# Cluster attention, experts and a bilinear layer on one core: expert order, small norms, last tile and a skipped branch

## The chip, the cores and the metric

The kernel runs on one core of a Trainium2 chip. The core has TensorE (matrix multiply; the profile shows matmuls as PE and weight loads as PEld), VectorE (DVE), ScalarE (ACT), GpSimd (POOL) and SyncE (SP), which only issues DMAs and handles semaphores here. Each engine works through its own queue of instructions in order; engines wait for one another by semaphores. The metric is the device time of one execution in microseconds.

## The reference

Three stages, all in float32. In the first, q and k (2 batches, 8 heads, 768 rows of 64) are given to the nearest of 16 centroids per head, and a row of q sees only rows of k of the same cluster.

```python
mask = q_assign[:, :, :, None] == k_assign[:, :, None, :]
scores = np.where(mask, scale * q @ k.T, -1e9)
attn = softmax(scores) ; x = attn @ v          # 1536 tokens x 512
expert_idx = argmax(normed(x) @ normed(expert_emb).T / tau)
gate = softmax(logits)[expert_idx]             # 8 experts
x = gate * (relu(x @ w1[e]) @ w2[e])           # each token by its expert e
out = ((x @ w_a) * (x @ w_b)) @ w_out          # 512 -> 1536 -> 512
```

## The kernel before

**Attention** goes over 8 pairs of heads in 96 steps of 128 query rows (SPP = 12 steps a pair). A step's scores go to PSUM, VectorE takes the row maximum (L601), ScalarE the exponential (L606), TensorE turns it (L621), ScalarE and VectorE copy it back (L625, L627), and after three steps the product with v follows (L648). Beside it, generators prepare the next pair: split_rows (with GpSimd's L389 and L390), prep_gen, and in the first pair setup_rest, which normalizes the expert embeddings.

A norm's reciprocal is made by `root_recip` (L265 to L286): three Newton rounds on a [rows, 1] column, each a reciprocal, a multiply by half (L279) and a multiply-add (L281), all on VectorE. It serves the centroids (128 rows), the embeddings (8 rows) and, on a 128x12 tile, the gates.

**Weights** come in chunks of 512x512. Chunks of turns with a wide tile go through four raw buffers of two quarter-chunks each: SP loads one (`load_raw`, L140 to L160), ScalarE makes the rounded high part (L207), VectorE the low part (L208), which frees the buffer. Chunks of the two narrow turns are loaded whole (`load_whole`, L172 to L180). The first four raw loads are issued during attention, at the steps of L872.

**Experts** are worked in eight turns. Expert 0 is the first turn; the others are ordered by how many tokens they have, and a turn's place in the order sets how wide its tile is (WIDTHS) and how many products it takes (KINDS). `ranks` (L1046) works the order out from the counts `cnt`: key, a comparison, its sum (pbase), then the table `at` and `turn_i`, the expert of each turn. SP reads turn_i into a register for the loads of later turns (L165), ScalarE for the gather of a turn's tokens (`load_xe`, L1134 to L1137). `limits` gives each expert's capacity and `most`, the largest overflow.

The main loop has an index G: 8 turns of 8 steps, then the bilinear layer. In a step TensorE does layer1(G) (L1169 in a wide turn) and layer2(G - 2) (L1286), ScalarE and VectorE make the hidden tile's two parts (L1246, L1247), and `split_some` splits as many quarter-chunks as a ramp and the room allow. At a turn's end the result ys is copied (L1299) and stored by SP (`put_rows`, L1310). Before the loop, the first turn's tile is taken from PSUM: cnt (L1017), two copies (L1020) and two subtractions (L1022).

At G = 5 stands `rare` (L1172): if an expert has more tokens than its turn's width, every engine goes through an arm that works the overflow in tiles of 128 tokens. All five engines load `most` into a register and branch (L1175). An engine that skips the arm goes through a short skipping arm instead: it waits for its own semaphores (and those of DMAs that it issued) to reach their count and adds what the arm would have added. With these inputs the arm is skipped. Its DMAs are issued by SP.

**Bilinear layer.** 1536 tokens in four chunks; at its end each 128-token tile is scaled by its gate and scattered to the output by GpSimd (`leave`, L1384 to L1397). The order of all instructions is the order in which this program writes them; no planner changes it.

Of the kernel before, what the change touches and what calls it, by code (L numbers as in the profile page):

```python
# [16 lines left out]
ALU = mybir.AluOpType  # L17
# [5 lines left out]
P = 128  # L23
# [25 lines left out]
def kernel(  # L49
# [215 lines left out]
    def root_recip(pool, shape, n2, name):  # L265

        g = pool.tile(shape, I32, name=name + "_g", bufs=1)
        nc.vector.tensor_scalar(out=g, in0=n2.bitcast(I32), scalar1=1, scalar2=None, op0=ALU.logical_shift_right)
        half = pool.tile(shape, F32, name=name + "_h", bufs=1)
        nc.vector.tensor_scalar(out=half, in0=n2, scalar1=0.5, scalar2=None, op0=ALU.mult)  # L270
        yield
        nc.vector.tensor_scalar(out=g, in0=g, scalar1=float(0x1FC00000), scalar2=None, op0=ALU.add)
        s0 = g.bitcast(F32)
        r = pool.tile(shape, F32, name=name + "_r", bufs=1)
        for _ in range(3):
            yield
            nc.vector.reciprocal(r, s0)
            yield
            nc.vector.tensor_mul(r, r, half)  # L279
            yield  # L280
            nc.vector.scalar_tensor_tensor(out=s0, in0=s0, scalar=0.5, in1=r, op0=ALU.mult, op1=ALU.add)  # L281
        yield
        nc.vector.tensor_scalar(out=s0, in0=s0, scalar1=1e-6, scalar2=None, op0=ALU.add)
        yield
        nc.vector.reciprocal(r, s0)
        return r  # L286
# [570 lines left out]
    for s in range(nst):  # L857
# [11 lines left out]
            nc.sync.dma_start(out=dst, in_=src)  # L869
        if i == SPP // 2 and pp > 0 and pp + 1 < NP:  # L870
            load_v(pp + 1)
        if s in (4 * SPP + 1, 4 * SPP + 3, 4 * SPP + 7, 4 * SPP + 9):  # L872
            load_raw()
        if s == (NP - 1) * SPP:
            near_open()
# [136 lines left out]
    def new_x(key, dt=F32R):  # L1012
        return big.tile([P, 2, DC, CAP], dt, tag="xT", name=f"xT_{key}", bufs=2)

    split_some(2)
    cnt = left.tile([P, NE, 1], F32, name="cnt")
    nc.vector.tensor_sub(cnt, cnt_p.rearrange("p (e o) -> p e o", o=1), ebase.rearrange("p o e -> p e o"))  # L1017
    xT_t[0] = new_x(0)
    for u in range(2):
        nc.scalar.copy(xT_t[0][:, 0, 2 * u:2 * u + 2, :], near_t["ps"][u])  # L1020
    for u in range(2):
        nc.vector.tensor_sub(xT_t[0][:, 1, 2 * u:2 * u + 2, :], near_t["ps"][u], xT_t[0][:, 0, 2 * u:2 * u + 2, :])  # L1022
    cnt_i = left.tile([1, NE], I32, name="cnt_i")
    most = left.tile([1, 1], I32, name="most")
    prod_ = left.tile([P, NE, OVM], F32, name="prod")
# [20 lines left out]
    def ranks():  # L1046

        nc.vector.scalar_tensor_tensor(out=key, in0=cnt.rearrange("p e o -> p o e"), scalar=float(NE), in1=iota_e, op0=ALU.mult, op1=ALU.add)
        nc.vector.memset(key[:, :, 0:1], float(2 ** 20))
        nc.vector.tensor_tensor(out=bef, in0=row(key), in1=col(key), op=ALU.is_gt)  # L1050
        nc.vector.tensor_reduce(out=pbase.rearrange("p o e -> p (o e)"), in_=bef, axis=AX.X, op=ALU.add)
        nc.vector.tensor_tensor(out=at, in0=row(rank_c), in1=col(pbase), op=ALU.is_equal)
        nc.vector.tensor_tensor(out=prod[0:1], in0=at[0:1].rearrange("p e q -> p q e"), in1=turn_c[0:1].to_broadcast([1, NE, NE]), op=ALU.mult)
        with nc.allow_low_precision(reason="whole numbers below 2^24"):
            nc.vector.tensor_reduce(out=turn_i[:, :NE], in_=prod[0:1], axis=AX.X, op=ALU.add)
            nc.vector.tensor_scalar(out=turn_i[:, NE:], in0=turn_i[:, :NE], scalar1=float(RX), scalar2=None, op0=ALU.mult)
        ranked.append(1)
# [9 lines left out]
    def further():  # L1067
# [10 lines left out]
        with nc.allow_low_precision(reason="whole numbers below 2^24"):  # L1078
# [3 lines left out]
            nc.vector.tensor_reduce(out=ov_i[:, 2 * NE:3 * NE], in_=ov_s, axis=AX.X, op=ALU.add)  # L1082
            nc.vector.tensor_tensor(out=ov_i[:, 3 * NE:], in0=ebase[0:1, 0, :], in1=cap[0:1, 0, :], op=ALU.add)
        nc.vector.tensor_copy(cnt_i, cnt[0:1, :, 0])

    ident = identr.bitcast(F32)
    psa_stack.close()
# [82 lines left out]


    def rare():  # L1172
        tc.mark_branch_hint_location("rare", "LikelyTaken", engines=[mybir.EngineType.PE])
        n_most = nc.values_load(most, min_val=0, max_val=NTOK)
        with tc.If(n_most > 0, label="rare"):  # L1175
            further()
            ovw = [big.tile([P, 2, 4, 512], F32, tag=f"w{NSLOT - 1 - c}", name=f"ov_w{c}") for c in range(2)]
            ovb_ = big.tile([P, 8, 512], F32, tag=f"w{NSLOT - 3}", name="ov_b")
# [7 lines left out]
            nc.vector.memset(yr, 0.0)  # L1186
            n_t = [nc.values_load(cnt_i[0:1, e:e + 1], min_val=0, max_val=NTOK) for e in range(NE)]
            for e in range(NE):
                i = nc.sync.dma_start(out=xs_d[bass.ds(n_t[e] + e * RX, P), :], in_=yr)
                if e == 0:  # L1190
                    for o in scatters:
                        tc.add_manual_dep(i.ins, o.name, DATA, reason="rows of every scatter")
            for e in range(NE):
# [1 line left out]
                row = nc.values_load(ov_i[0:1, e:e + 1], min_val=0, max_val=NTOK)  # L1195
                first = nc.values_load(ov_i[0:1, 3 * NE + e:3 * NE + e + 1], min_val=e * RX, max_val=e * RX + CAP)
                with tc.For_i(0, n_e, 1) as it:
                    nc.sync.dma_start(out=xr, in_=xs_d[bass.ds(nc.s_assert_within(first + it * P, min_val=e * RX, max_val=e * RX + NTOK), P), :])
                    for c in range(FF // 512):
                        for z in range(2):  # L1200
                            nc.sync.dma_start(out=ovw[c][:, z], in_=chunks[4 * e + 2 * c + z])
                    for j in range(DC):
                        nc.tensor.transpose(pt[:, j, :], xr[:, j * P:(j + 1) * P], ident)
                    nc.vector.tensor_copy(xrT, pt)
                    for c in range(FF // 512):
                        for f in range(4):
                            for j in range(DC):
                                nc.tensor.matmul(ph[:, f, :], ovw[c][:, 0, j, f * P:(f + 1) * P], xrT[:, j, :], start=(j == 0), stop=(j == DC - 1))
                        nc.vector.tensor_scalar(out=hT[:, 4 * c:4 * c + 4, :], in0=ph, scalar1=0.0, scalar2=None, op0=ALU.max)
                    for c in range(FF // 512):  # L1210
                        for f in range(4):
                            for j in range(DC):
                                nc.tensor.matmul(pt[:, j, :], ovw[c][:, 1, f, j * P:(j + 1) * P], hT[:, 4 * c + f, :],
                                                 start=(c == 0 and f == 0 and j == 0), stop=(c == FF // 512 - 1 and f == 3 and j == DC - 1))
                    nc.vector.tensor_copy(yr, py)
                    nc.sync.dma_start(out=ys_v[:, :, bass.ds(nc.s_assert_within(row + it * P, min_val=0, max_val=NTOK), P)],
                                      in_=yr.rearrange("p (j t) -> p j t", t=P))


# [164 lines left out]
    def leave(ck, t):  # L1384
        at = CHUNKS[ck][0] // P + t
        ot = big.tile([P, DM], F32, tag="a", name=f"ot_{at}", bufs=NA)
        g2 = res[:, at, 1:2].bitcast(F32)
        if t % 2:
            nc.scalar.activation(ot, o_ps[ck][t], AF.Copy, scale=g2)
        else:  # L1390
            nc.vector.tensor_scalar(out=ot, in0=o_ps[ck][t], scalar1=g2, scalar2=None, op0=ALU.mult)
# [41 lines left out]
    for G in range(total_f + tot + LAG):  # L1433
# [3 lines left out]
        room = 4 * (NSLOT + 2 * (max(G - LAG, 0) // 4)) - nsplit[0]  # L1437
        if 4 * NCE <= nsplit[0] and I < 0 and G % NF > 1:
            narrow_a(min(room, 1))
        if G == 1:  # L1440
            ranks()
        if G == 2:
            limits()
        if G == GR:
# [1 line left out]
        if I < 0:  # L1446
# [2 lines left out]
                load_xe(1 if G == 2 else 2)  # L1449
            if G == NF:  # L1450
                further()
            if G == GR - 2:
                tc.mark_branch_hint_location("rare", "LikelyTaken", engines=[mybir.EngineType.DVE])
            e, f = divmod(G, NF)
            if 2 * NF <= G < 3 * NF:
                next(rr, None)
# [26 lines left out]
        elif I < 0:  # L1483
            narrow_c()
            narrow_b(1)
            narrow_d()
        if G == GR - 1:
            tc.mark_branch_hint_location("rare", "LikelyTaken", engines=[mybir.EngineType.SP])


# [28 lines left out]
```

## Time and profile before

| | us |
|---|---|
| median of 3 runs (lowest, highest) | 772.91 (771.47, 772.96) |
| the profiled execution | 772.48 |
| its span, first to last instruction | 770.4 |
| TensorE matmul busy | 749.1 (97%) |
| VectorE busy | 465.4 (60%) |
| ScalarE busy | 374.2 (49%) |
| GpSimd busy | 106.0 (14%) |

TensorE's granted clock is full in all 40 slices. Attention takes the first 290 us or so, the eight turns up to about 460, the bilinear layer the rest. DMA moves 91.87 MB, a mean of 119 GB/s, and is busiest in the slices from 310 to 440 us. A matmul's end is modelled in the profile, so that two in a row overlap a little; idle time in brackets is counted from that end.

### The profile page before, as it was taken

What the parts mean: (1) busy time and instruction counts of PE and PEld (TensorE: products, weight loads), DVE (VectorE), ACT (ScalarE), POOL (GpSimd) and SP (SyncE); (2) the same over time, 40 slices, a digit from 0 to 9 for tenths busy, and PEclk for the clock granted to TensorE, in tenths of its full rate; (3) what the DMA queues carried; (4) which work ended last, traced back from release to release, by engine and by line L of the source; (5) the groups of instructions that cost most, each with busy time, mean ns of one, the idle gap of its engine ahead of it and who ended that gap; (6) DMA issues with size and microseconds to landing.
All of it is one profiled execution on the core that took longest, in us unless ns stands there. A gap on an engine that the chain in (4) does not pass through costs nothing.

```text
span 770.4 us, 12666 instructions
## 1 busy us (share of the span) xinstructions
PE 749.1 (97%) x4777; PEld 629.4 (82%) x4777; DVE 465.4 (60%) x911; ACT 374.2 (49%) x769; POOL 106.0 (14%) x145
## 2 busy tenths in 40 slices
PE   8989999999999998999999999999999999999996
PEld 5667777767777668999999999888898888888996
DVE  7877676787767666477876799686653121121211
ACT  5666766678666674366655555344323121111211
POOL 6303203052200040000000003222001020000201
PEclk9999999999999999999999999999999999999999
DMA  6327223163121036789879877464411010000100
GB/s 187 85 85 266 48 76 85 59 199 100 46 48 32 28 110 202 275 310 294 274 235 255 284 229 235 113 138 112 134 29 55 1 55 1 1 0 1 55 1 28
DMA packets 48132, 91.87 MB, mean 119 GB/s; under 512 B 6328, under 2 KB 20280, under 8 KB 48064
## 3 DMA queue, kind: packets, MB, share of 16 engines
q1 hardware_dynamic: 43856, 81.01, 34.9%
q0 software_dynamic: 2304, 6.31, 2.1%
q10 hardware_dynamic: 1904, 3.67, 1.4%
q8 instruction: 39, 0.64, 0.3%
q14 instruction: 29, 0.24, 0.1%
HBM read 69.27 MB, written 14.04 MB: 108 GB/s over the span
## 4 chain that ended last, share of the span: by engine, by line
issue 28%; PE 23%; DMA 4%; DVE 2%; POOL 1%; ACT 1%; SPq 0%; POOLq 0%; ACTq 0%; DVEq 0%
PE ab L1169 7%; PE y L1286 4%; PE y L1290 2%; PE h L1250 2%; DMA raw<-in_moe_w_dram 2%; PE h L1169 2%; PE h L1242 2%; PE o_sc L1414 1%; DMA ys_d<-ys 1%; PE y L1291 1%; PE h L1251 1%; POOL out_dram L1392 1%; DVE w L208 1%; ACT w L207 1%; PE o_pp L1414 1%
## 5 line engine op out<-in xcount | busy, mean ns | idle before, releaser
L1373 DVE TENSOR_TENSOR ga<-ab,ga 128x256 f32<-128x256 f32 (+1 forms) x48 | 26.7, 557 | 156.8 <-PE ab L1169 111.0
L1169 PE MATMUL ab<-xT_b,w 128*128 128x256 f32 (+1 forms) x720 | 113.2, 305 | 0.0
L606 ACT ACTIVATE E<-sc,nmx 128x768 f32<-128x768 f32 x96 | 86.7, 903 | 54.0 <-DVE nmx L601 42.1
L1169 PE MATMUL ab<-x,w 128*128 128x512 f32 x432 | 108.1, 390 | 0.0
L1169 PEld LDWEIGHTS ab<-xT_b,w 128*128 128x128 f32 x720 | 98.6, 190 | 7.2
L601 DVE TENSOR_REDUCE nmx<-sc 128x1 f32<-128x768 f32 x96 | 91.4, 953 | 7.6 <-PE sc L593 6.5
L1169 PEld LDWEIGHTS ab<-x,w 128*128 128x128 f32 x432 | 81.1, 188 | 17.2
L621 PEld LDWEIGHTS et<-ident,E 128*128 128x128 f32 x576 | 62.3, 140 | 34.6 <-ACT ET L625 14.4
L621 PE MATMUL et<-ident,E 128*128 128x128 f32 x576 | 82.3, 279 | 4.2 <-ACT E L606 1.7
L627 DVE COPY ET<-et 128x384 f32<-128x384 f32 x96 | 52.6, 548 | 53.7 <-PE et L621 50.8
L1372 ACT COPY ga<-ab 128x256 f32<-128x256 f32 (+1 forms) x48 | 23.0, 480 | 126.9 <-PE ab L1169 123.8
L592 PE MATMUL sc<-K,Q 80*128 80x512 f32 x192 | 72.9, 380 | 1.4 <-DMA Q<-ohT 1.1
L648 PE MATMUL pv<-ET,v 128*64 128x384 f32 (+2 forms) x408 | 73.0, 479 | 0.6 <-ACT ET L625 0.5
L208 DVE TENSOR_TENSOR w<-raw,w 128x1024 fp32r<-128x1024 f32 x48 | 58.1, 1219 | 21.1 <-ACT w L207 20.5
L1414 PE MATMUL o_sc<-w,g 128*128 128x512 f32 x288 | 69.5, 390 | 0.0
L1374 ACT CAST g<-ga 128x256 fp32r<-128x256 f32 (+1 forms) x48 | 24.7, 514 | 84.1 <-DVE ga L1373 84.1
L1414 PEld LDWEIGHTS o_sc<-w,g 128*128 128x128 f32 x288 | 53.9, 188 | 11.3
L593 PE MATMUL sc<-K,Q 128*128 128x512 f32 x192 | 61.2, 340 | 0.0
L1286 PE MATMUL y<-hh,w 128*128 128x256 f32 (+3 forms) x416 | 59.3, 290 | 0.0
L207 ACT CAST w<-raw 128x1024 fp32r<-128x1024 f32 x48 | 50.3, 1049 | 18.5 <-DMA raw<-in_moe_w_dram 11.7
L1286 PEld LDWEIGHTS y<-hh,w 128*128 128x128 f32 x416 | 54.4, 190 | 0.3 <-DVE ys L1260 0.3
L625 ACT COPY ET<-et 128x384 f32<-128x384 f32 x96 | 45.6, 475 | 2.6 <-PE et L621 2.6
(268 smaller groups left out, 1204.0 us busy)
## 6 DMA issues: line engine op xcount, KB each, us to landing
raw<-in_moe_w_dram SPq DMA_DIRECT2D x48, 512.0 KB
w<-in_moe_w_dram SPq DMA_DIRECT2D x16, 512.0 KB
raw<-in_moe_w_a_dram SPq DMA_DIRECT2D x12, 512.0 KB
raw<-in_moe_w_b_dram SPq DMA_DIRECT2D x12, 512.0 KB
raw<-in_moe_w_out_dram SPq DMA_DIRECT2D x12, 512.0 KB
xs_d<-zero SPq DMA_DIRECT2D x8, 512.0 KB
xe<-xs_d ACTq DMA_DIRECT2D x7, 512.0 KB
v<-in_v_dram SPq DMA_DIRECT2D x8, 384.0 KB
```

The costliest lines, as they stand in the source:

```text
L207: nc.scalar.copy(hi, w)
L208: nc.vector.tensor_sub(lo, w, hi)
L592: nc.tensor.matmul(ps[:, lo:hi], Q3[:, qs], K3[:, h * S + lo:h * S + hi], start=True, stop=False)
L593: nc.tensor.matmul(ps[:, lo:hi], Q2[:, qs], K2[:, h * S + lo:h * S + hi], start=False, stop=True)
L601: nc.vector.tensor_reduce(out=nmx[pp][:, h, t:t + 1], in_=sc[s], axis=AX.X, op=ALU.max, negate=True)
L606: nc.scalar.activation(e, sc.pop(s), AF.Exp, bias=nmx[pp][:, h, t:t + 1], accum_out=sums[pp][:, t, h:h + 1])
L621: nc.tensor.transpose(pt[:, j * P:(j + 1) * P], e[:, kt * P:(kt + 1) * P], ident)
L627: nc.vector.tensor_copy(dst, src)
L648: nc.tensor.matmul(pv[h * D:(h + 1) * D, :], vt[:, h, kt, :], ets[g, h][:, kt, :n * P], start=(kt == 0), stop=(kt == NT - 1))
L1169: nc.tensor.matmul(ps, s_, m_, start=(i == 0), stop=(i == len(ops) - 1))
L1286: nc.tensor.matmul(ys_ps[e][j // 2][:, j % 2, :wd], w[:, m_, ff, j * P:(j + 1) * P], s_, start=(f == 0 and i == 0 and j % 2 == 0), stop=(l ...
L1414: nc.tensor.matmul(o_ps[ck][t], s_[:, t * P:(t + 1) * P], w_[:, m_], start=(f == 0 and i == 0), stop=(J == I and f == NF2 - 1 and i == 2))
```

## The change

Five edits. `root_recip` takes the multiply and the multiply-add of a [rows, 1] column as operations of one tensor with a per-partition scalar. The fourth raw load goes from step 4 SPP + 9 to 5 SPP + 3. `ranks` becomes a generator: its first four instructions are issued after cnt and ahead of the split and the tile of the first turn, the other four behind that tile, in place of G = 1. The rare arm's DMAs are issued by GpSimd, the branch prefers the skipping arm as the block that follows it, and three branch hints go. The last output tile is scaled in halves, one by ScalarE and one by VectorE.

```diff
--- before.py
+++ after.py
@@ -276,9 +276,15 @@
             yield
             nc.vector.reciprocal(r, s0)
             yield
-            nc.vector.tensor_mul(r, r, half)
+            if shape[1] == 1:
+                nc.vector.tensor_scalar(out=r, in0=r, scalar1=half, scalar2=None, op0=ALU.mult)
+            else:
+                nc.vector.tensor_mul(r, r, half)
             yield
-            nc.vector.scalar_tensor_tensor(out=s0, in0=s0, scalar=0.5, in1=r, op0=ALU.mult, op1=ALU.add)
+            if shape[1] == 1:
+                nc.vector.tensor_scalar(out=s0, in0=s0, scalar1=0.5, scalar2=r, op0=ALU.mult, op1=ALU.add)
+            else:
+                nc.vector.scalar_tensor_tensor(out=s0, in0=s0, scalar=0.5, in1=r, op0=ALU.mult, op1=ALU.add)
         yield
         nc.vector.tensor_scalar(out=s0, in0=s0, scalar1=1e-6, scalar2=None, op0=ALU.add)
         yield
@@ -869,7 +875,7 @@
             nc.sync.dma_start(out=dst, in_=src)
         if i == SPP // 2 and pp > 0 and pp + 1 < NP:
             load_v(pp + 1)
-        if s in (4 * SPP + 1, 4 * SPP + 3, 4 * SPP + 7, 4 * SPP + 9):
+        if s in (4 * SPP + 1, 4 * SPP + 3, 4 * SPP + 7, 5 * SPP + 3):
             load_raw()
         if s == (NP - 1) * SPP:
             near_open()
@@ -1012,14 +1018,8 @@
     def new_x(key, dt=F32R):
         return big.tile([P, 2, DC, CAP], dt, tag="xT", name=f"xT_{key}", bufs=2)
 
-    split_some(2)
     cnt = left.tile([P, NE, 1], F32, name="cnt")
     nc.vector.tensor_sub(cnt, cnt_p.rearrange("p (e o) -> p e o", o=1), ebase.rearrange("p o e -> p e o"))
-    xT_t[0] = new_x(0)
-    for u in range(2):
-        nc.scalar.copy(xT_t[0][:, 0, 2 * u:2 * u + 2, :], near_t["ps"][u])
-    for u in range(2):
-        nc.vector.tensor_sub(xT_t[0][:, 1, 2 * u:2 * u + 2, :], near_t["ps"][u], xT_t[0][:, 0, 2 * u:2 * u + 2, :])
     cnt_i = left.tile([1, NE], I32, name="cnt_i")
     most = left.tile([1, 1], I32, name="most")
     prod_ = left.tile([P, NE, OVM], F32, name="prod")
@@ -1049,6 +1049,7 @@
         nc.vector.memset(key[:, :, 0:1], float(2 ** 20))
         nc.vector.tensor_tensor(out=bef, in0=row(key), in1=col(key), op=ALU.is_gt)
         nc.vector.tensor_reduce(out=pbase.rearrange("p o e -> p (o e)"), in_=bef, axis=AX.X, op=ALU.add)
+        yield
         nc.vector.tensor_tensor(out=at, in0=row(rank_c), in1=col(pbase), op=ALU.is_equal)
         nc.vector.tensor_tensor(out=prod[0:1], in0=at[0:1].rearrange("p e q -> p q e"), in1=turn_c[0:1].to_broadcast([1, NE, NE]), op=ALU.mult)
         with nc.allow_low_precision(reason="whole numbers below 2^24"):
@@ -1082,6 +1083,16 @@
             nc.vector.tensor_reduce(out=ov_i[:, 2 * NE:3 * NE], in_=ov_s, axis=AX.X, op=ALU.add)
             nc.vector.tensor_tensor(out=ov_i[:, 3 * NE:], in0=ebase[0:1, 0, :], in1=cap[0:1, 0, :], op=ALU.add)
         nc.vector.tensor_copy(cnt_i, cnt[0:1, :, 0])
+
+    rk = ranks()
+    next(rk)
+    split_some(2)
+    xT_t[0] = new_x(0)
+    for u in range(2):
+        nc.scalar.copy(xT_t[0][:, 0, 2 * u:2 * u + 2, :], near_t["ps"][u])
+    for u in range(2):
+        nc.vector.tensor_sub(xT_t[0][:, 1, 2 * u:2 * u + 2, :], near_t["ps"][u], xT_t[0][:, 0, 2 * u:2 * u + 2, :])
+    next(rk, None)
 
     ident = identr.bitcast(F32)
     psa_stack.close()
@@ -1170,9 +1181,8 @@
 
 
     def rare():
-        tc.mark_branch_hint_location("rare", "LikelyTaken", engines=[mybir.EngineType.PE])
         n_most = nc.values_load(most, min_val=0, max_val=NTOK)
-        with tc.If(n_most > 0, label="rare"):
+        with tc.If(n_most > 0, label="rare", preferred_fallthrough_block=False):
             further()
             ovw = [big.tile([P, 2, 4, 512], F32, tag=f"w{NSLOT - 1 - c}", name=f"ov_w{c}") for c in range(2)]
             ovb_ = big.tile([P, 8, 512], F32, tag=f"w{NSLOT - 3}", name="ov_b")
@@ -1186,7 +1196,7 @@
             nc.vector.memset(yr, 0.0)
             n_t = [nc.values_load(cnt_i[0:1, e:e + 1], min_val=0, max_val=NTOK) for e in range(NE)]
             for e in range(NE):
-                i = nc.sync.dma_start(out=xs_d[bass.ds(n_t[e] + e * RX, P), :], in_=yr)
+                i = nc.gpsimd.dma_start(out=xs_d[bass.ds(n_t[e] + e * RX, P), :], in_=yr)
                 if e == 0:
                     for o in scatters:
                         tc.add_manual_dep(i.ins, o.name, DATA, reason="rows of every scatter")
@@ -1195,10 +1205,10 @@
                 row = nc.values_load(ov_i[0:1, e:e + 1], min_val=0, max_val=NTOK)
                 first = nc.values_load(ov_i[0:1, 3 * NE + e:3 * NE + e + 1], min_val=e * RX, max_val=e * RX + CAP)
                 with tc.For_i(0, n_e, 1) as it:
-                    nc.sync.dma_start(out=xr, in_=xs_d[bass.ds(nc.s_assert_within(first + it * P, min_val=e * RX, max_val=e * RX + NTOK), P), :])
+                    nc.gpsimd.dma_start(out=xr, in_=xs_d[bass.ds(nc.s_assert_within(first + it * P, min_val=e * RX, max_val=e * RX + NTOK), P), :])
                     for c in range(FF // 512):
                         for z in range(2):
-                            nc.sync.dma_start(out=ovw[c][:, z], in_=chunks[4 * e + 2 * c + z])
+                            nc.gpsimd.dma_start(out=ovw[c][:, z], in_=chunks[4 * e + 2 * c + z])
                     for j in range(DC):
                         nc.tensor.transpose(pt[:, j, :], xr[:, j * P:(j + 1) * P], ident)
                     nc.vector.tensor_copy(xrT, pt)
@@ -1213,7 +1223,7 @@
                                 nc.tensor.matmul(pt[:, j, :], ovw[c][:, 1, f, j * P:(j + 1) * P], hT[:, 4 * c + f, :],
                                                  start=(c == 0 and f == 0 and j == 0), stop=(c == FF // 512 - 1 and f == 3 and j == DC - 1))
                     nc.vector.tensor_copy(yr, py)
-                    nc.sync.dma_start(out=ys_v[:, :, bass.ds(nc.s_assert_within(row + it * P, min_val=0, max_val=NTOK), P)],
+                    nc.gpsimd.dma_start(out=ys_v[:, :, bass.ds(nc.s_assert_within(row + it * P, min_val=0, max_val=NTOK), P)],
                                       in_=yr.rearrange("p (j t) -> p j t", t=P))
 
 
@@ -1385,7 +1395,10 @@
         at = CHUNKS[ck][0] // P + t
         ot = big.tile([P, DM], F32, tag="a", name=f"ot_{at}", bufs=NA)
         g2 = res[:, at, 1:2].bitcast(F32)
-        if t % 2:
+        if at == NTOK // P - 1:
+            nc.scalar.activation(ot[:, :DM // 2], o_ps[ck][t][:, :DM // 2], AF.Copy, scale=g2)
+            nc.vector.tensor_scalar(out=ot[:, DM // 2:], in0=o_ps[ck][t][:, DM // 2:], scalar1=g2, scalar2=None, op0=ALU.mult)
+        elif t % 2:
             nc.scalar.activation(ot, o_ps[ck][t], AF.Copy, scale=g2)
         else:
             nc.vector.tensor_scalar(out=ot, in0=o_ps[ck][t], scalar1=g2, scalar2=None, op0=ALU.mult)
@@ -1437,8 +1450,6 @@
         room = 4 * (NSLOT + 2 * (max(G - LAG, 0) // 4)) - nsplit[0]
         if 4 * NCE <= nsplit[0] and I < 0 and G % NF > 1:
             narrow_a(min(room, 1))
-        if G == 1:
-            ranks()
         if G == 2:
             limits()
         if G == GR:
@@ -1449,8 +1460,6 @@
                 load_xe(1 if G == 2 else 2)
             if G == NF:
                 further()
-            if G == GR - 2:
-                tc.mark_branch_hint_location("rare", "LikelyTaken", engines=[mybir.EngineType.DVE])
             e, f = divmod(G, NF)
             if 2 * NF <= G < 3 * NF:
                 next(rr, None)
@@ -1484,8 +1493,6 @@
             narrow_c()
             narrow_b(1)
             narrow_d()
-        if G == GR - 1:
-            tc.mark_branch_hint_location("rare", "LikelyTaken", engines=[mybir.EngineType.SP])
 
 
 # ---- launch: one core; inputs and outputs as the reference has them ----
```

## Rows read from the trace of the kernel before

**Rows 1.** TensorE's waits over the span: total us, times, longest us.
```profile
PE h L1169 <- DVE cnt L1017: 1.2, 1, 1.2
PE et L621 <- DVE sv L449: 1.1, 1, 1.1
```

**Rows 2.** timeline, all engines, 286 to 308: start us, length us, engine, line.
```profile
289.72 1.23 DVE L208 TENSOR_TENSOR w<-raw,w 128x1024 fp32r<-128x1024 f32 x1 [1.61 <-ACT w L207]
...
290.94 1.30 DVE L1022 TENSOR_TENSOR xT<-xT_near,xT 128x512 fp32r<-128x512 f32 x2
...
291.17 4.38 PE L1169 MATMUL h<-xT,w 128*128 128x256 f32 x36 [1.19 <-DVE cnt L1017]
...
295.39 0.16 DVE L1048 SCALAR_TENSOR_TENSOR key<-cnt,iota_e 128x8 f32<-128x8 f32 x1
...
296.22 0.22 DVE L1052 TENSOR_TENSOR at<-rank_c,pbase 128x64 f32<-128x64 f32 x1
...
297.02 0.16 DVE L1056 TENSOR_SCALAR turn_i<-turn_i 1x8 int32<-1x8 int32 x1
...
298.24 1.60 PE L1286 MATMUL y<-hh,w 128*128 128x256 f32 x12
...
299.35 1.05 ACT L207 CAST w<-raw 128x1024 fp32r<-128x1024 f32 x1 [3.38 <-DVE held L1063]
...
299.68 1.16 PE L1169 MATMUL h<-xT,w 128*128 128x256 f32 x5
...
302.65 1.60 PE L1286 MATMUL y<-hh,w 128*128 128x256 f32 x12
```

**Rows 3.** timeline of TensorE, 336 to 369, the places with idle time.
```profile
342.14 1.70 PE L1169 MATMUL h<-xT,w 128*128 128x256 f32 x12 [1.36 <-DVE hh L1247]
...
354.92 1.70 PE L1169 MATMUL h<-xT,w 128*128 128x256 f32 x12 [0.40 <-DVE hh L1247]
...
367.03 0.47 PE L1290 MATMUL y<-hh,w 128*128 128x448 f32 x1 [1.06 <-DVE ys L1299]
```

**Rows 4.** chain of waits, 316 to 368: start us, length us, what.
```profile
320.54 9.47 DMA ys_d<-ys
...
334.52 4.91 DMA raw<-in_moe_w_dram
```

**Rows 5.** timeline of SP's queue, 296 to 336.
```profile
305.65 1.05 SPq L156 DMA_DIRECT2D raw<-in_moe_w_dram  x1
316.83 2.20 SPq L180 DMA_DIRECT2D w<-in_moe_w_dram  x4
```

**Rows 6.** the branch's line: engine, operation, count, ns, first and last start.
```profile
L1175 SPq EVENT_SEMAPHORE  x9: 17/17/17, 311.4 to 316.3; - x9
...
L1175 POOLq COMPARE_BRANCH  x1: 53/53/53, 300.2 to 300.2; - x1
...
L1175 POOLq EVENT_SEMAPHORE  x1: 17/17/17, 304.6 to 304.6; - x1
L1175 SPq COMPARE_BRANCH  x1: 70/70/70, 307.4 to 307.4; - x1
```

**Rows 7.** windows: busy us by engine, TensorE's clock, DMA share, GB/s.
```profile
312.00:318.00 6.00, 6.00 (x50) 6.00 (x49) 3.58 (x18) 0.92 (x3) 0.00 (x0) 1.00 0.30 97
318.00:342.00 24.00, 22.78 (x178) 22.58 (x176) 13.72 (x17) 14.21 (x23) 0.00 (x0) 1.00 0.95 336
```

**Rows 8.** line of the norms' multiply: ns min/median/max, starts.
```profile
L279 DVE TENSOR_TENSOR c_r<-c_r,c_h x3: 158/159/292, 3.8 to 6.4; 128x1 f32<-128x1 f32 x3
L279 DVE TENSOR_TENSOR e_r<-e_r,e_h x3: 136/137/1387, 35.6 to 44.4; 8x1 f32<-8x1 f32 x3
```

**Rows 9.** timeline, all engines, 33.5 to 46.
```profile
35.15 1.82 POOL L390 TENSOR_TENSOR qr<-q,qr 128x768 fp32r<-128x768 f32 x1
```

**Rows 10.** timeline of GpSimd at the end of the span.
```profile
764.97 0.09 POOL L1397 MEMSET tick<- 1x1 f32 x1
765.30 0.96 POOL L1392 DMA_INDIRECT out_dram<-ot,res  x1 [0.25 <-ACT ot L1389]
```

## The prediction

> **What bounds the kernel now.** First the table of engines: TensorE is busy for nearly the whole span, so only what makes it wait, or what it does at the very ends, can move the time. Second the waits of TensorE [rows 1] and its timeline where they lie. Four places matter, and each hangs on another engine. (1) At 37.6 us it waits 1.1 us for VectorE's sv [rows 1]. (2) At 291.17, the start of the first expert turn, it waits for cnt [rows 2]. (3) In the group of 12 matmuls that starts at 299.68 it waits for a weight split: the next group starts 2.97 us later, against 1.44 us between 298.24 and 299.68 for an undisturbed group, so 1.53 us are lost [rows 2]. (4) At 342.14, 354.92 and 367.03 it waits 1.36, 0.40 and 1.06 us for VectorE [rows 3]; the chain of waits follows these back to raw weights that land late (4.91 us from issue at 334.52) and to one store, ys at 320.54, that takes 9.47 us to land while ScalarE's next gather stands behind it [rows 4].
>
> The queue view says why the weights are late. SP ends an issue at 306.70 (305.65 + 1.05) and issues nothing until 316.83 [rows 5]. In between stand its branch at 307.4, then nothing to 311.4, and nine semaphore events up to 316.3 [rows 6]: 4.0 us to get to the skipping arm, 4.9 us in it, where SP waits for its own transfers in flight so as to count up the semaphores of DMAs that the skipped arm would have issued. The windows show the price: from 312 to 318 the DMA engines are 30% busy, after that 95% until 342 [rows 7]. So some 4.2 us of transfer time (0.7 of 6) are lost just before the stage in which weights are short.
>
> **The change part by part.** The sum is made against the profiled execution, 772.48 us (770.4 of span and 2.1 around it); the median of the runs shown is 0.43 above it.
>
> *Skipping arm and its DMAs, stream: -2.9.* The rare arm's four DMA statements leave SP's queue for GpSimd's, so SP's skipping arm has its register load to count and no transfer to wait for. SP's next four whole-chunk loads (L180) and the raw load behind them move from 316.83 to about 308, the store ys finds an emptier queue, and ScalarE's gather with the splits behind it follows. The stream gains about the 4.2 us of the bubble; the raw loads that end the waits of [rows 3] need 1.4 to 2.5. Those three waits are 2.82 us by the modelled ends; a matmul's modelled end outlasts the next start by 0.16 (a group is 1.60 long, the next starts after 1.44 [rows 2]), so 3.3 in all. I keep 0.4 because TensorE comes there 2 us earlier itself. Ends: 0 (the splits are late for another reason) and -3.3. GpSimd's queue takes the semaphores over; it passes its branch at 300.2 and is in its arm at 304.6 [rows 6]. Behind the arm stand only the scatters of the gates, two turns later, so its waits cost nothing there; SP's and ScalarE's transfers, which must now wait for GpSimd's counts, get them 12 us ahead of 316.83.
>
> *Experts ordered ahead of the first turn: -1.53 + 0.55.* VectorE's eight instructions take 1.79 us from 295.39 to 297.18 [rows 2]. ScalarE's gather of turn 1 needs their result, and its split at 299.35 stands behind that gather after 3.38 us of idling [rows 2]. With the order known by about 293.9 (292.24, 0.66 of delay and 0.96 for the last four, both below), ScalarE goes on at once; the split comes at least 1.2 us earlier, its VectorE half is no longer behind 1.79 us of small work, and the 1.53 at (3) goes (ends: -0.5 and -1.53). The price is at 290. The first four instructions (0.83 from 295.39 to 296.22) and cnt now stand ahead of the split at 289.72. VectorE idles 1.61 us before it, but cnt's matmul ends late in that idle time; I let a third of the work fit and take 0.66 of delay for the split and the two subtractions that end at 292.24 [rows 2]. TensorE starts without waiting for cnt, then stops at its eleventh matmul, which reads the second subtraction; it did so at about 291.17 + 10 x 0.12 = 292.4, so 0.1 is slack: +0.55. Ends: -0.3 (all fits) and +0.9 (none does). The last four (296.22 to 297.18) go where VectorE has only the first hh to do, which TensorE reads two groups later; without that room they would cost their 0.96. SP's and ScalarE's register loads of turn numbers find theirs ready; the raw load behind SP's is bound by a split and gains that split's advance only.
>
> *Norms by scalars: -1.1.* One two-input multiply on 8x1 takes 1387 ns where the others take 137; the 128x1 one takes 292 against 159 [rows 8]. The long one starts at 35.6 and ends at 36.98, with GpSimd's two-input subtraction, 35.15 + 1.82 = 36.97 [rows 9]: VectorE stood still for 1.25 us, and sv, for which TensorE waits 1.1 us at (1), was next in its queue. The new form has one tensor and one per-partition scalar. No row shows that form beside such a GpSimd operation; ends 0 and -1.25. I take -1.0, since TensorE then waits for ScalarE's exponential instead (-0.1), and VectorE is the late engine through the next steps, so the gain is not lost again. The centroid chain, which ends in TensorE's first real work, gets 0.13 of its 292 back: -0.1. The other ten keep about their 0.14 to 0.16 us [rows 8], and the gates' norm keeps the old form.
>
> The Trainium skill, SBUF — State Buffer, section Who interferes with whom, has it that a VectorE instruction with two SBUF inputs contends with a GpSimd instruction that reads SBUF, and that one with at most one such input does not. The trace agrees on the first half (1387 against 137 ns); on whether a per-partition scalar counts as an input it is silent. If it does not count, the term would be -1.4 by the rule and the sum 767.6.
>
> *Last tile in halves: 0.* ScalarE's half copy would be some 0.3 us shorter, but GpSimd's queue is the end: its memset of the tile before ends at 765.06 and the last scatter starts at 765.30 with 0.25 idle [rows 10]. The last scatter now waits for two engines; behind it stand one memset and the end. Ends: 0 and -0.24 (765.30 less 765.06). *One raw load six steps later: 0.* It leaves its place behind one pair's small loads in SP's queue and goes in ahead of the next load of v; its buffer is first read in the first turn, after two more pairs of heads, which hide its landing. Without that cover its 4.91 us [rows 4] would show. *Hints gone:* no cost in the forecast, since the skipping arm follows the branch; see the second rival.
>
> Sum: -2.9 - 1.53 + 0.55 - 1.1 = -5.0: 767.5 against the profiled run, 767.9 beside the median.
>
> **The rivals.** *Splits late for their own sake, 770.8.* ScalarE and VectorE are loaded in this stage, and a ramp of three parts a step may keep DMA at its limit whenever it starts; then the 2.9 stay. Against it: 318 to 342 is transfer-bound at 95% and starts with a backlog [rows 7]. Chance 0.17.
>
> *The jump moves to TensorE, 772.1.* If the skipping arm comes first and the rare arm next, the skipping arm must end in a jump over the rare arm's 8 x 68 matmuls and their weight loads, now without a hint. Engines that had to fetch stood 4.0 us (SP) and 4.4 us (GpSimd) [rows 6]; TensorE is drained there, so it would pay about 4.2 in full: 767.9 + 4.2. For it: both pages missed after one branch. Against: one that is laid out to fall through needs no jump. Chance 0.15. The Trainium skill, Runtime: NRT & Kernel Launch, section Instruction fetch mechanics, says that "A taken branch whose target isn't in the current 2-page window forces a DMA fetch of the target page before execution can continue"; SP's 4.0 us agree, for TensorE no run here shows it.
>
> *The other side, 775.1.* The same place, but TensorE's sequential fetch of the rare arm is in flight first and the right page queues behind it: 4.2 + 3.0 = 7.2, an estimate that adds most of one more fetch to the 4.2. It turns the result from 6.6 us on (above 774.5). Nothing in the trace shows two such fetches in a row. Chance 0.08.
>
> That the scalar form does not free VectorE gives 768.9 and lies in the forecast's own range; unknown mishaps have 0.08.
>
> **How the numbers follow.** Forecast 0.52, own range 766.2 to 769.8. About 0.2% (1.5 us) is what a measurement of this kernel can tell from no change. Faster: 0.52, most of the 0.17, and 0.04 of the rest: 0.71. Same: the jump's 0.12, and parts of the others: 0.18. Slower: 0.11. The range begins where all terms are at their far ends (-3.3 - 1.53 - 0.3 - 1.38 - 0.24 = -6.75, so 766.2, and a little below for the terms' own error) and goes up to the jump in full with 0.9 to spare: 766.0 to 773.0.
>
> **What would show it.** Right: SP's issues of L180 near 308, DMA busy through 312 to 318, no TensorE idle at 342 to 367, ys landing in about 3 us, no 1.39 us multiply near 35.6, the group after 299.68 at 1.44 us. The start of the turn right if TensorE's first group of 12 is longer than 1.6 us. Wrong: an idle TensorE of several us at the branch; waits on raw loads as before; a GpSimd arm that SP's loads wait for.

## The result: slower, and where the time went

The changed kernel takes 778.86 us (median of 5, 776.78 to 780.22) against 771.47 for the kernel before beside it: a ratio of 1.0089, 95% interval 1.0070 to 1.0108 (the two medians alone give 1.0096). The forecast was 767.9. The profiled execution took 779.52, its span 778.0. Of the page of after, the rows of TensorE's busy time, its granted clock and DMA, in 40 slices where there are digits ("..." in a view stands for rows left out):

```profile
PE 754.4 (97%) x4777; PEld 633.2 (81%) x4777; DVE 464.8 (60%) x912; ACT 374.3 (48%) x769; POOL 106.1 (14%) x145
...
PEclk8999999999999999899999999999999999999999
DMA  6237133162221037669978886555411010000100
```

TensorE is busy for the same share as before, but the clock row now has two slices at 8, the first and the seventeenth (311 to 331 us). The waits of TensorE over the whole span begin with one that the kernel before does not have:

```profile
PE h L1180 <- issue: 7.6, 1, 7.6
```

"issue" means that it waited for nothing that the profile shows. Its timeline gives the place:

```profile
303.42 1.60 PE L1296 MATMUL y<-hh,w 128*128 128x256 f32 x12
312.61 2.93 PE L1180 MATMUL h<-xT,w 128*128 128x256 f32 x12 [7.59 <-issue]
```

The group at 312.61 takes 2.93 us, a group of the same 12 matmuls at 299.12 took 1.58. The instructions of the branch (L1185) say what lies in the gap (count, shortest/median/longest in ns, first and last start):

```profile
L1185 PEldq COMPARE_BRANCH  x2: 95/3642/7190, 303.3 to 305.4; - x2
...
L1185 PEldq EVENT_SEMAPHORE  x2: 51/51/51, 305.1 to 305.2; - x2
L1185 SPq COMPARE_BRANCH  x2: 41/47/53, 307.9 to 308.1; - x2
L1185 POOLq INC_SWDGE_SEM  x1: 412/412/412, 301.2 to 301.2; - x1
...
L1185 SPq EVENT_SEMAPHORE  x1: 17/17/17, 308.0 to 308.0; - x1
```

Before, each engine had one COMPARE_BRANCH; now there are two. The first (95 ns on TensorE) leads to the skipping arm, whose two semaphore events come when the last group of matmuls is done; the arm is over at 305.3, and the second, the jump over the rare arm, takes 7190 ns with TensorE idle. The windows show the clock after it (columns: stretch, its length, busy us and count of PE, PEld, DVE, ACT, POOL, then the granted clock, the DMA share, GB/s):

```profile
12.00:22.00 10.00, 10.00 (x40) 6.78 (x39) 5.01 (x10) 3.45 (x8) 6.59 (x4) 0.50 0.57 167
...
309.00:315.00 6.00, 2.40 (x11) 2.40 (x12) 0.00 (x0) 0.00 (x0) 0.00 (x0) 0.50 0.82 293
316.00:322.00 6.00, 6.00 (x55) 6.00 (x54) 2.46 (x4) 1.70 (x3) 0.00 (x0) 1.00 0.52 173
```

After idling, TensorE works at 1.2 GHz (0.50) until about 316, at 2.4 again from there. Matmul by matmul against the trace before, the delay goes from 0.8 us ahead of the branch to 8.1 behind it and 9.5 when the clock is back. (The stretch from 12 to 22 at 1.2 GHz belongs to this single execution: see the last section.)

SP was to be free at 308. Its arm is short, but then it jumps too, and its next instruction starts at 315.08. Behind that it reads the semaphores that GpSimd counts up, and 1.95 us pass between two of these reads (315.25 and 317.20). GpSimd had counted them by 301.7 (its INC_SWDGE_SEM above), so this is no wait for GpSimd, though two of the expectations below take it for one; what SP stood for there is open. Its issues:

```profile
306.37 0.81 SPq L156 DMA_DIRECT2D raw<-in_moe_w_dram  x1
317.54 2.77 SPq L180 DMA_DIRECT2D w<-in_moe_w_dram  x4
```

L180 at 317.54 stands against 316.83 in [rows 5]. The other edits did act. At the first turn, the clock at 2.4 GHz, TensorE before:

```profile
289.71 0.28 PE L792 MATMUL xT_near<-oneh,x_near_lo 128*128 128x256 f32 x1
...
295.38 1.60 PE L1286 MATMUL y<-hh,w 128*128 128x256 f32 x12
```

and after:

```profile
291.86 0.28 PE L798 MATMUL xT_near<-oneh,x_near_lo 128*128 128x256 f32 x1
292.33 1.23 PE L1180 MATMUL h<-xT,w 128*128 128x256 f32 x8 [0.20 <-ACT xT L1092]
293.92 3.93 PE L1180 MATMUL h<-xT,w 128*128 128x256 f32 x28 [0.36 <-DVE xT L1094]
297.69 1.60 PE L1296 MATMUL y<-hh,w 128*128 128x256 f32 x12
```

The wait for cnt of [rows 2] (1.19 us) is gone, and TensorE stops for the tile's copies and subtractions instead. The two nearly cancel: it is 2.15 us later than before ahead of the turn (291.86 against 289.71) and 2.31 at the first group for y (297.69 against 295.38), so the start costs 0.16. The stall of the group after 299.68 is gone: at the next group for y the delay is 0.77 (303.42 against 302.65 in [rows 2]), so 1.54 us are won back. The norms:

```profile
L280 DVE TENSOR_SCALAR c_r<-c_r,c_h x3: 213/214/215, 4.0 to 6.4; 128x1 f32<-128x1 f32 x3
L280 DVE TENSOR_SCALAR e_r<-e_r,e_h x3: 192/193/193, 39.5 to 47.2; 8x1 f32<-8x1 f32 x3
```

None takes 1387 ns now, but each is 55 ns longer than in [rows 8] (193 against 137, 214 against 159). The tail, from the last tiles on:

```profile
772.15 0.48 DVE L1400 TENSOR_SCALAR ot<-o_pv,res 128x256 f32<-128x256 f32 x1 [1.11 <-ACT ot L1399]
...
772.91 0.96 POOL L1405 DMA_INDIRECT out_dram<-ot,res  x1 [0.55 <-DVE ot L1400]
```

VectorE's half is released by ScalarE's, so the halves run one after the other. From TensorE's last start to the end of the span it is 6.79 us; before 6.48. With that the account of the two spans closes: 2.15 us ahead of the first turn, -1.38 there, 7.29 at the branch, 1.40 by the clock behind it, -2.17 in the turns up to 367 of the trace before, 0.31 at the end, 7.60 in all (778.0 less 770.4).

### The profile page after: what moved, and what is told of

The parts are those of the page before. It is cut to its first block, busy times and chain, and to the rows that moved or that the text cites. A ratio compares the mean times of both kernels' runs of the same rounds, so it can differ in the third digit from the quotient of the medians.

```text
span 778.0 us, 12682 instructions
## 1 busy us (share of the span) xinstructions
PE 754.4 (97%) x4777; PEld 633.2 (81%) x4777; DVE 464.8 (60%) x912; ACT 374.3 (48%) x769; POOL 106.1 (14%) x145
## 4 chain that ended last, share of the span: by engine, by line
issue 29%; PE 25%; DVE 3%; DMA 2%; POOL 1%; ACT 0%; POOLq 0%; SPq 0%; DVEq 0%; ACTq 0%
PE ab L1180 6%; PE y L1296 4%; PE h L1260 3%; PE y L1300 2%; PE h L1180 2%; PE h L1252 2%; DMA raw<-in_moe_w_dram 2%; PE o_sc L1427 1%; PE h L1261 1%; PE y L1301 1%; DVE w L208 1%; POOL out_dram L1405 1%; PE o_pp L1427 1%; PE o_pv L1427 1%; DMA res<-tab_d 0%
## 5 line engine op out<-in xcount | busy, mean ns | idle before, releaser
L1180 PE MATMUL h<-xT,w 128*128 128x256 f32 (+1 forms) x288 | 40.0, 289 | 9.0 <-issue 7.6
```

Of the source, the lines that this page charges most:

```text
L1180: nc.tensor.matmul(ps, s_, m_, start=(i == 0), stop=(i == len(ops) - 1))
```

## The experiments

Theory 1: the loss is TensorE's jump over the rare arm. Rival: the DMAs on GpSimd. Ratios are to the kernel before, run beside each; where us stand for a ratio, they are its difference from 1 times 771.5.

**e1_old_layout.** Everything of the change but the branch.

```diff
-        with tc.If(n_most > 0, label="rare", preferred_fallthrough_block=False):
+        tc.mark_branch_hint_location("rare", "LikelyTaken", engines=[mybir.EngineType.PE])
+        ...  (and the hints of VectorE and SP)
+        with tc.If(n_most > 0, label="rare"):
```

> The changed kernel, but with the branch laid out as before (rare arm behind the branch, the skipping arm at its end) and the three hints back; the rare arm's DMAs stay on GpSimd. Theory 1 (the loss is TensorE's jump over the rare arm: its second branch instruction took 7.19 us, the clock after it about 1.1 more): TensorE reaches the skipping arm in one branch of about 2 us as before, and the time falls by 7.2 to 8.5 from 778.9, to 770.4 to 771.7; if SP is then also freed early, as the prediction had it, to about 768. Rival (the loss comes with the DMAs on GpSimd, whose counts SP waited for until 317.4): stays above 776.

768.16 us, ratio 0.9952 (0.9930 to 0.9973): faster than before by 3.7 us, with the DMAs on GpSimd. The rival falls. TensorE's one branch:

```profile
L1186 PEldq COMPARE_BRANCH  x1: 388/388/388, 299.8 to 299.8; - x1
...
L1186 SPq COMPARE_BRANCH  x1: 70/70/70, 304.1 to 304.1; - x1
L1186 SPq EVENT_SEMAPHORE  x1: 17/17/17, 308.2 to 308.2; - x1
```

SP still stands 4.1 us at its branch, as in [rows 6], but its arm holds one event: L180 follows at 308.85, and the DMA engines are 92% busy in a stretch in which they were 30% busy before [rows 7]:

```profile
312.00:318.00 6.00, 6.00 (x50) 6.00 (x49) 2.80 (x13) 1.50 (x4) 0.00 (x0) 1.00 0.92 335
```

Of the waits of [rows 3] 0.2 us are left, in one line of TensorE's waits from 290 to 400:

```profile
PE h L1180 <- DVE hh L1258: 0.2, 1, 0.2
```

**e2_layout_alone.** The kernel before with `preferred_fallthrough_block=False` and no hints.

> The kernel before with the new layout of the branch alone (skipping arm first, hints gone); the rare arm's DMAs stay on SP. Theory 1: TensorE and SP each stand about 7 us at a second branch instruction; 771.5 + 7.2 to 8.5 = 778.7 to 780. SP is then later than in the changed kernel (7.0 us and then its own wait for its transfers, 4.9 us), so it may be more. Rival (GpSimd's DMAs): 771.5, no change.

779.32 us, 1.0098 (1.0064 to 1.0132). The edit of the branch, without the moved DMAs and the rest, makes the loss; TensorE's second branch takes 6470 ns:

```profile
L1174 PEldq COMPARE_BRANCH  x2: 95/3282/6470, 301.5 to 303.5; - x2
```

**e5_one_expert_arm.** The changed kernel, with a rare arm for the first expert alone.

```diff
-            for e in range(NE):
+            for e in range(1):
                 n_e = nc.values_load(...)
```

> The changed kernel with a rare arm that works the overflow of the first expert alone, not of all eight (none overflows with these inputs): TensorE's part of the arm shrinks from 8 x 68 matmuls with their weight loads to 68. Theory 1 in its form that the price is the fetch of a far target: TensorE's second branch costs under 2 us in place of 7.19, the time is 770 to 772. Rival: the price of the second branch does not hang on the distance: 778 to 779, 7 us at the branch.

768.71 us, 0.9960 (0.9942 to 0.9977), below the 770 to 772 expected. The layout and the jump are still there; only the code jumped over is shorter, and TensorE's jump costs 310 ns:

```profile
L1185 PEldq COMPARE_BRANCH  x2: 95/202/310, 303.7 to 305.7; - x2
```

So neither the second branch nor the layout as such costs 7 us, but the length of the code jumped over. SP's jump is short here too, and for once SP is free when the prediction wanted it:

```profile
308.71 2.68 SPq L180 DMA_DIRECT2D w<-in_moe_w_dram  x4
```

Still e5 is not faster than e1, where SP stood 4.1 us, and TensorE waits 1.2 us for hh and ys from 290 to 400 in its trace.

**e6_unhinted.** The kernel before without its three hints.

> The kernel before with its three branch hints taken out and nothing else (rare arm behind the branch, skipping arm at its end: TensorE, skipping, still jumps over the rare arm). Theory 1a (a far jump costs TensorE about 7 us when nothing has announced it; in the kernel before the hint had paid for it): TensorE stands 6.5 to 7.2 us at its one branch, 771.5 + 7 to 8.5 = 778 to 780. Theory 1b (it is the new layout that makes the far jump, the hint is worth nothing): TensorE's branch stays at 0.4 us, 771 to 772.

776.59 us, 1.0057 (1.0035 to 1.0079): 1a, though less than its 778 to 780 and 6.5 to 7.2 us. The kernel before also jumps over the rare arm, to its skipping arm; only the hint had made that cheap. The kernel before:

```profile
L1175 PEldq COMPARE_BRANCH  x1: 397/397/397, 302.6 to 302.6; - x1
```

and e6:

```profile
L1174 PEldq COMPARE_BRANCH  x1: 5072/5072/5072, 303.6 to 303.6; - x1
```

Part of the 5.07 us is hidden, as the branch starts while TensorE still has a group of matmuls to work off. In TensorE's waits the idle time is less:

```profile
PE h L1169 <- PEq L1174: 3.7, 1, 3.7
```

In the new layout the long jump stands behind the skipping arm, which waits for these matmuls, so all of it shows. Why the jump itself takes 5.07 us here, 6.29 (e13) to 7.21 (e7) there, is open.

**e7_layout_with_hints.** The changed kernel with the three hints.

> The changed kernel with the three hints back, the new layout kept. Theory 1a: if the hint serves whichever branch follows its mark, the second branch is cheap again and the time is 768 to 770; if it serves the first branch's target alone (the rare arm), TensorE still stands 7 us at the second: 778 to 780. Theory 1b: 778 to 780.

781.06 us, 1.0102 (1.0069 to 1.0134), the second case of 1a or 1b, a little above their range. In the new layout the hint does nothing for the second branch:

```profile
L1186 PEldq COMPARE_BRANCH  x2: 104/3656/7209, 303.9 to 305.9; - x2
```

**e3_gpsimd_dmas.** The kernel before, `nc.sync.dma_start` to `nc.gpsimd.dma_start` in the rare arm.

> The kernel before with the rare arm's four DMA statements on GpSimd alone; layout and hints as before. The prediction's step: SP issues its next whole-chunk loads at about 308 in place of 316.83, the three waits at 342 to 367 go, 771.5 - 2.9 = 768.6. Rival A: SP waits for GpSimd's counts, its loads stay at 316 or later: 771 to 772. Rival B (GpSimd's DMAs are the loss): above 775.

771.30 us, 0.9989 (0.9971 to 1.0006): a gain of 0.8 us at best estimate, not the 2.9, and none is not excluded. Some 0.6 of it lies outside the span: the time less the span is 1.44 to 1.57 us in every execution with these DMAs on GpSimd, 2.02 to 2.16 with them on SP in the old layout. SP's loads moved only to

```profile
312.69 2.80 SPq L180 DMA_DIRECT2D w<-in_moe_w_dram  x4
```

because the 3.9 us at SP's branch (308.1 to 312.0) stay. TensorE's waits for hh from 290 to 400 fall from 1.8 to

```profile
PE h L1169 <- DVE hh L1247: 1.2, 2, 1.0
```

and the one for ys (1.1, [rows 3]) goes.

**e8_sp_dmas** and **e13_layout_sp_dmas.** The DMAs back on SP, in e1's layout and in the changed kernel's.

> e1_old_layout (old layout, hints, all the rest of the change: 768.2) with the rare arm's DMAs back on SP. The prediction's stream term of 2.9 would make it 771.1. Rival (what the kernel before with GpSimd's DMAs alone showed, 0.2): 768.2 to 769; SP's loads at about 313 to 316 all the same, and the waits at 342 to 367 as before.

> The changed kernel with the rare arm's DMAs back on SP, the new layout kept. Theory: in the changed kernel SP's own second branch (7.0 us) and its wait for GpSimd's counts (until 317.4) had eaten what the moved DMAs gave, so this runs like it: 778.5 to 779.5. Rival: the moved DMAs gave their 2 us there too: 780.5 to 781.5.

e8: 770.22 us, 0.9978 (0.9962 to 0.9995), so in the old layout the moved DMAs are worth about 2 us against e1, with intervals that overlap. The traces agree: from 302.65 to 367.03 of the trace before, TensorE gains 2.5 us on it in e1 and 1.0 in e8, and 0.6 lies outside the span. e13: 777.99 us, 1.0101 (1.0072 to 1.0130), against the changed kernel's 1.0089 (1.0070 to 1.0108): in the new layout they are worth nothing that can be measured. A reason that fits, though no run isolates it: while TensorE stands at its jump, weights catch up that it would have waited for (in e13, with the DMAs on SP, its waits for hh from 290 to 400 are 0.3 us).

**e9_old_norms, e10_old_ranks, e11_norm_multiply.** e1 without the new norms, without the new place of ranks, and with the scalar form in one multiply (8 rows) alone.

> e1_old_layout (768.2) with the old form of the norms. The prediction's term of 1.1 would make it 769.3, with a two-input multiply of 1.2 to 1.4 us near 35.6 and a wait of TensorE for sv. Rival (VectorE is early again a few steps on, or the scalar form's 55 ns more in each of twelve operations eats it): 768 to 768.5.

> e1_old_layout (768.2) with ranks at its old place, G = 1. The prediction's terms, -1.53 and +0.55, would make it 769.2: the group after 299.68 stalls for 1.5 us again, the start of the first turn is 0.5 us earlier. Rival (the delay of the first turn's tile eats the whole gain, since in the profile of e1 the first turn starts 1.0 us later against the kernel before): 768 to 768.4.

> e1_old_layout (768.2) with the scalar form for the multiply of the embeddings (8 rows) alone; the multiply-add and all of the centroids' chain as before. If the gain of the norms, 2.9 us, is the one long multiply (1.4 us near 35.6) and what follows from it, it stays: 768, or 0.1 less for the centroids' chain. If the centroids or the multiply-adds carry it: 769 to 771.

0.9997 (0.9983 to 1.0011), 0.9998 (0.9980 to 1.0017) and 0.9985 (0.9970 to 1.0000): against e1 they lose 3.5, 3.6 and 2.5 us. That is more than the terms say, and with the 2 of e8 far more than the 3.7 that e1 gains in all, so not all of them can be right. e11's 770.36 us lie where its expectation put the case that the centroids or the multiply-adds carry the gain; its trace says otherwise, as no multiply of it is long (192 ns) and one multiply-add takes 361. The long multiply is back in e9:

```profile
L279 DVE TENSOR_TENSOR e_r<-e_r,e_h x3: 138/138/1401, 35.9 to 44.7; 8x1 f32<-8x1 f32 x3
```

**e16_norms_alone, e17_ranks_alone**, run on one chip with e14 and e15, to settle these sizes.

> The kernel before with the norms by scalars and nothing else. The prediction's term: 1.1 us less, 0.9986 of the kernel before. If the 2.9 us that their loss cost in e9 stand by themselves: 0.9962. If the gain needs the other parts: 0.9995 to 1.

> The kernel before with the experts ordered ahead and nothing else. The prediction's terms: 1.0 us less, 0.9987. If the 3.6 of e10 stand by themselves: 0.9953. If the first turn's later start eats it: 1.

Norms: 771.00, 0.9982 (0.9965 to 1.0000), a gain of 1.4 us, with none at the interval's end. Ranks: 771.07, 0.9992 (0.9974 to 1.0011), 0.6 us, with no gain inside the interval. With 0.8 of e3 that is 2.8 us, about as much as e14 below (2.5), which has all three and the moved raw load. Why e9 lost more stays open; it ran on e1's chip. For e10 the clock is part of it: 8 of its 12 executions had a mean granted clock below 0.995, against 4 of the 29 of the kernel before on that chip, and in its trace the clock falls at 12.5 and 53.5 us, far ahead of the place that e10 changes. Within like clocks (the groups of the last section) e10 is 1.7 to 2.1 us faster than the kernel before, e1 3.5 to 3.8.

**e12_sp_mark_old_tail, e14_old_tail, e15_keep_clock.** Versions meant to beat both.

```diff
 e14 = e1 with the last tile in one piece; e12 = e14 and
-            if G == GR - 1: SP's hint
+            if G == GR - 2: SP's hint, with VectorE's
 e15 = e14 and
-        keep_warm(wps[:, :512], 3)
+        keep_warm(wps[:, :512], 5)
...
-    keep_warm(wps[:, :512], 1)
+    keep_warm(wps[:, :512], 2)
```

> A version meant to beat both: e1_old_layout with the last tile in one piece as before (in the traces its halves ran one after the other and the span's end came 0.31 us later), and SP's branch hint one step earlier, with VectorE's. Expected: 0.3 from the tail; if the earlier hint has the page in time, SP passes its branch in under 1 us in place of 4.1 and issues L180 near 305 in place of 308.8: 0 to 1 us more. 767 to 767.9. Rival: the hint's place does not matter, SP stands 4 us: 767.9.

> e1_old_layout (0.9952 of the kernel before) with the last tile in one piece, as before. The halves ran one after the other in the traces, 0.31 us in all: 0.9948 of the kernel before. Rival: the end is set elsewhere, 0.9952.

> e14_old_tail with three more matmuls on ones between 6 and 9 us, where TensorE is idle for some 0.6 us while it waits for the centroids. If that idle time is what lets the granted clock fall to 1.2 GHz at about 12 us in some executions, none of them shows it, and the median falls by about 1 us against e14_old_tail. Rival: the clock falls as often as before; the median is the same or 0.2 us higher.

e12: 769.40, 0.9963 (0.9946 to 0.9979), not the 767 to 767.9 expected; from its branch at 306.65 to its arm SP stands 3.4 us, and L180 goes out at 310.72. In the other kernels of this layout with hints it is 3.8 to 4.4, so the earlier place helps little, and not to under 1 us. e14: 769.67, 0.9967 (0.9948 to 0.9987). e15: 768.44, 0.9953 (0.9935 to 0.9972). All three beat both kernels, as e1 does. Among e1, e12, e14 and e15 the intervals overlap; the tail's 0.31 us is seen in the traces and is too small for them.

## Why the prediction was wrong

**The step that failed** is the one on the hints: "*Hints gone:* no cost in the forecast, since the skipping arm follows the branch". The arm does follow, but it must end in a jump to the code behind the rare arm. The second and third rival had said so, and were given 0.15 and 0.08. Two things spoke for them ahead of the result: [rows 6], with engines that stood 4.0 to 4.4 us, should have raised the question why TensorE's single branch passed in 0.4 us (its hint, as e6 with 5.07 showed later); and the rare arm's 8 x 68 matmuls are there for every layout to jump over. What the runs showed in place of no cost is 7.19 us at the jump and 1.40 at 1.2 GHz behind it. The third rival's price of 7.2 us met the 7.19 measured, though what makes it (it was put down to two fetches in a row) no row shows. Even that rival gave 775.1 where 778.9 was measured: it left out those 1.4 us at 1.2 GHz, and it counted the other edits' gain at 5.0 in full, of which the runs show 2.5 to 3.7.

The rule cited there from the Trainium skill, Runtime: NRT & Kernel Launch, section Instruction fetch mechanics, that a taken branch out of the pages at hand forces a fetch before execution goes on, agrees with the runs: 7.19 us over eight experts' code, 0.31 over one's.

**Stream, -2.9.** The path was right and the size was not. SP was to be free at 308; that needs a jump that costs nothing, as in e5. Old layout: the branch holds SP for 3.9 to 4.1 us as before, L180 comes 4.1 us earlier in e3, DMA is busy through 312 to 318 (e1), and the gain is 0.8 us alone, about 2 in e1, 0.6 of either outside the span, for which the prediction had no term. The waits were also larger in the one trace that the term was read from: hh and ys cost TensorE 2.9 us there from 290 to 400, and 1.3, 1.7 and 1.8 in e8, e16 and e17, which have the rare arm's DMAs and the layout as before. New layout: SP stands 7.0 us at the second branch, L180 is not earlier at all. The three waits of [rows 3] are all but gone in after too (0.7 us in all from 316 to 400), yet likely for another reason: TensorE came 9.5 us later.

**Experts ahead, -1.53 + 0.55.** Mechanism and size were right. In the trace of after the stall gives 1.54 and the start takes 0.16, -1.4 in all; counted the same way, e17's trace has 1.54 and 0.40. By the time e17 gains 0.6 us, with an interval that includes both none and the forecast's 1.0. The first turn waits for copies as well as the subtractions.

**Norms, -1.1.** Right in kind, 1.4 us alone. "The other ten keep about their 0.14 to 0.16 us" was wrong by 55 ns each. The centroids' chain, from its first reciprocal to csq, took 3.47 us in place of 3.58, the 0.1 of the forecast; it ended 0.1 us later in after, as it had begun 0.2 later. The collision went in spite of the longer form. In e16 GpSimd's two-input subtraction and the new multiply beside it:

```profile
35.11 1.82 POOL L396 TENSOR_TENSOR qr<-q,qr 128x768 fp32r<-128x768 f32 x1
...
35.54 0.19 DVE L280 TENSOR_SCALAR e_r<-e_r,e_h 8x1 f32<-8x1 f32 x1
```

So a per-partition scalar does not count as a second input here, the half of the rule in the Trainium skill, SBUF — State Buffer, section Who interferes with whom, on which the trace before was silent. That page says it of instructions outside VectorE's two-port modes, a condition that the prediction left out.

**Last tile, 0 (ends 0 and -0.24).** Outside its ends on the other side: +0.31, since the halves run in turn (0.47 + 0.48 us in place of 0.69, and a wait between them).

**The raw load, 0.** No run takes it alone.

Without the branch's layout the sum of the runs is about -1.4 - 0.8 - 0.6 + 0.3 = -2.5 where the forecast had -5.0, and e1, at -3.7 (2.1 to 5.4), holds both within its interval. The sign of the whole was decided by the one edit that was costed at nothing.

## What to carry to other kernels

A conditional arm that is never run still has to be passed: for each engine ask which of its instructions lie between the branch and the code behind, whether one path jumps over them, and whether a hint stands for just that jump. Cost it on the engine that bounds the kernel, drained, with the clock's recovery behind it; the jump over an arm that is short on that engine (e5) cost 0.31 us. And an edit costed at nothing because something "follows directly" needs its end followed as well as its start. A term that is read from the waits of one trace should be checked against a second one: here the same waits were 2.9 us in one and 1.3 to 1.8 in three others.

## What the runs showed of the hardware besides

The jump's price hung on the engine: in after, from the second branch to the next instruction, TensorE 7.2 us, SP 7.0, GpSimd 4.0, ScalarE 0.5. In e5 it was 0.4, 0.2, 0.5 and 0.2. It is not fixed for an engine either: SP's was 5.5 in e7 and 2.7 in e13. Hints paid for TensorE's jump in the old layout (0.39 against 5.07 us) and, by one trace of it, for VectorE's (0.6 us from branch to arm in the kernel before, 5.2 in e6); SP stood 3.4 to 4.4 us with its hint and 5.7 without in e6, so there it paid for a part at most.

In some executions the granted clock falls to 1.2 GHz within the first 25 us, in some (e8, e10, e13, e16) between 50 and 57. In after TensorE had been busy for 6.2 of the 7 us ahead of that (5 to 12 us); in e1, where it did not fall, for 6.4. It is in the profile of after (12 to 22, above) and of e17, not in that of before, and not in those of e1, e14 and e15. Of 35 executions of the kernel before on one chip, the 20 with a mean clock of 0.998 or more had a median of 770.96 us, the 9 from 0.995 to 0.997 772.36, the 6 below that 774.30. Three more matmuls in TensorE's idle time at 6 to 9 us (e15) left 7 of 12 executions in the first group against 2 of 12 (e14) on the same chip; with the kernel before at 20 of 35 that is not yet shown to be the cause. A profiled pair of executions can thus differ by 3 us at the start that no edit made: ahead of the first turn, where e17 has nothing changed yet, its trace is 3.0 us behind that of before.
